# Attention in longer runs of one kind of matmul, earlier loads, an even spread of row transposes in an auction

## The chip, the cores and the metric

The kernel runs on one core of a Trainium2 chip. The metric is the time of one execution on the device, in microseconds (us); lower is better. The five engines work side by side and are tied together by semaphores: TensorE (PE in the rows; PEld is its weight load), VectorE (DVE), ScalarE (ACT), GpSimd (POOL) and SyncE (SP), which issues most of the DMAs.

## The reference, cut to what matters

```python
def _attn_ref(q, k, v):                     # 4 batches, 12 heads, 448 positions, 64 wide
    scores = scale * np.matmul(q, k.transpose(0, 1, 3, 2)) - np.log(S)
    attn = 1.0 / (1.0 + np.exp(-scores))
    return np.matmul(attn, v)

def _moe_ref(x, w_gate, w1, w2):            # 1792 tokens of 768, 8 experts of 1024
    logits = x @ w_gate
    # all (token, expert) pairs in falling order of logit: a token goes to the expert of the first
    # pair at which it is free and the expert has fewer than 224 tokens
    ...
    out[mask] = np.maximum(x[mask] @ w1[e], 0.0) @ w2[e]

def _moe2_ref(x, w_in, w_out, s, b):        # one dense layer, 768 to 2048 and back
    r = np.maximum(x @ w_in, 0.0)
    return (s * (r * r) + b) @ w_out
```

The three run one after the other, in float32.

## The kernel before, in words

Three stages follow each other. **Attention** fills the first 181 us. Heads go in pairs: 4 batches of 6 pairs make 24 pairs, and the pair number i runs from 0 to 23. For a pair the kernel loads `rk` and `rq` (keys and queries, transposed; `load_qk`) and `vt` (values; `load_v`). The 448 keys are cut into 4 chunks `c` of 112. For a chunk PE makes two score matmuls, one for each head, into a two-bank tile `psc` (line 237; 64 contraction rows and 112 output columns of the array each, and the two heads use the upper and the lower half of its rows), and ACT takes the sigmoid into `attn` (line 238). The product with the values adds the 4 chunks up in one bank `pv` (line 243; 112 rows and 64 columns, the two heads use the two halves of the columns), and ACT copies it to `xT` (line 252). A matmul of float32 is two instructions on PE, so "x8" in a row is four matmuls.

The function `scores_av(n, i, mid)` makes the scores of pair n = i + 1 and the values of pair i together. It alternates: the scores of two chunks (four matmuls), then the values of two chunks (four matmuls), and so once more. One call is called a round here. The callback `mid` puts the router's small matmuls between: `gate` (line 259) adds up the logits of a batch in the bank `plg`, ACT copies them to `lg` (line 264), `gate_turn` (line 271) turns them into the bank `pt`, and `prefs` on DVE (lines 280 to 287) copies them to `L` and ranks them. In the last batch `bracket` finds the range of the logits in three stages, with two more small matmuls (lines 297 and 303) into `plg`.

Beside that, DVE narrows the second layer's weights from int64 pairs to float32: `convert` is four DVE instructions (lines 155 to 158) on one of 32 pieces, `CONV[i]` of them after round i. A piece is loaded into one of three buffers `craw`, and its result `co` (three buffers too) is stored to `nw` one conversion later. In the last four rounds ACT and POOL split the first pieces of the experts' weights (`w_high`, line 187; `w_low`, line 198).

All these loads and stores are issued by SP, in the order of the program. A load waits on SP until its buffer is free, and everything behind it waits too. The loads of pair i + 3 (q, k) and i + 2 (v) are issued at round i.

**The auction** (181 to 217 us) gives tokens to experts: `STEPS` = 10 steps of prices, each a chain DVE (`aw`), PE (`pa`), DVE (`LM`), comparisons on DVE and on ACT (line 456), PE (`pb`), DVE (`jd`). PE and ACT use the gaps to turn `xT` into rows: one turn is four transposes into `px` (line 409), an ACT copy to `xrow` (line 416) and a store to `xs` (line 417). There are 24 turns: one before the steps, `ROWS[it]` in each step, and what is left in `places`, which builds the lists `idx` of tokens (matmuls of line 525, and line 529). The first `SYNC` = 4 turns are stored from ACT's queue, the rest from SP's. **The experts** and the dense layer take the rest, from a gather of the rows (line 539) on.

Of the kernel before, what the change touches and what calls it, by code (L numbers as in the profile page):

```python
# [8 lines left out]
F32 = mybir.dt.float32  # L9
# [15 lines left out]
CP = 112  # L25
# [12 lines left out]
MORE = (3, 8)  # L38
AHEAD = (2, 3, 4, 5)
WARM = (9, 10)  # L40
ROWS = (2, 2, 2, 3, 3, 3, 2, 2, 2, 2)
SYNC = 4
SIGNS = 2
CONV = [1, 1, 2, 1, 2] * 4 + [1, 2, 1]
FULL = CAP - 0.5
BIG = 1.0e30
FLATC = 16384.0
# [14 lines left out]
def tile_kernel(ctx, tc, qT, kT, v, wg, w1, w2, wi, wo, s2, b2, cst, out):  # L62
# [53 lines left out]
    cgp = early.enter_context(tc.tile_pool(name="cgp", bufs=1))  # L116

    att = ExitStack()
    qk = att.enter_context(tc.tile_pool(name="qk", bufs=4))
    vp = att.enter_context(tc.tile_pool(name="vp", bufs=2))  # L120
    at = att.enter_context(tc.tile_pool(name="at", bufs=2))
    ps_s = att.enter_context(tc.tile_pool(name="ps_s", bufs=2, space=PSUM))
    ps_v = att.enter_context(tc.tile_pool(name="ps_v", bufs=2, space=PSUM))
    ps_l = att.enter_context(tc.tile_pool(name="ps_l", bufs=1, space=PSUM))


# [20 lines left out]
    def convert():  # L147
        if not coming:
            return
        i = coming.pop(0)  # L150
        r = craw.pop(i)
        lo, hi = r[:, :, 0], r[:, :, 1]
        b = cgp.tile([128, 768], I32, name="cb_", bufs=2)
        a = cgp.tile([128, 768], I32, name="co", bufs=3)
        V.tensor_scalar(a, hi, 3, 0x3FFFFFFF, op0=ALU.logical_shift_left, op1=ALU.bitwise_and)
        V.tensor_scalar(b, lo.bitcast(U32), 2.0 ** -29, None, op0=ALU.mult)
        V.scalar_tensor_tensor(a, hi, -(1 << 30), a, op0=ALU.bitwise_and, op1=ALU.bitwise_or)
        V.tensor_tensor(a, a, b, op=ALU.add)
        cout.append((i, a))
        cv_out(1)  # L160
        cv_in()
# [47 lines left out]

    def load_v(i):  # L210
        b, p = pairs[i]
        vt[i] = vp.tile([CP, NC, 128], F32, name="vt", bufs=4)
        nc.sync.dma_start(vt[i], v[b, p])

    def load_qk(i):
# [4 lines left out]
        nc.sync.dma_start(rq, qT[b, p])  # L220
        raw_qk[i] = (rq, rk)

    def scores_av(n, i, mid):
        if n is not None:
            rq, rk = raw_qk.pop(n)
            attn[n] = at.tile([CP, 2, NC, S], F32, name="attn")
        if i is not None:
            a = attn.pop(i)
            pv = ps_v.tile([128, 512], F32, name="pv")
        for c2 in range(0, NC, 2):  # L230
            for c in (c2, c2 + 1):
                mid(c)
                if n is not None:
                    p = ps_s.tile([CP, 2, 512], F32, name="psc")
                    for j in range(2):
                        me = slice(j * D, (j + 1) * D)
                        T.matmul(p[:, j, :S], rk[me, c * CP:(c + 1) * CP], rq[me], start=True, stop=True)  # L237
                    A.activation(attn[n][:, :, c, :], p[:, :, :S], AF.Sigmoid, bias=nls[:CP],  # L238
                                 scale=1.0 / math.sqrt(D))
            for c in (c2, c2 + 1):  # L240
                if i is not None:
                    for j in range(2):
                        T.matmul(pv[j * 64:(j + 1) * 64, :S], vt[i][:, c, j * D:(j + 1) * D], a[:, j, c, :],  # L243
                                 start=(c == 0), stop=(c == NC - 1))
        if i is not None:
            b, p = pairs[i]
            xt = xT[:, p, b * S:(b + 1) * S]
            if i == len(pairs) - 1:
                A.copy(xt[:, :2 * CP], pv[:, :2 * CP])
                A.copy(xt[:, 2 * CP:], pv[:, 2 * CP:S])  # L250
            else:
                A.copy(xt, pv[:, :S])

    def gate(b, p0, p1, last):
        if p0 == 0:
            plg[b] = ps_l.tile([128, 512], F32, name="plg")
        for p in range(p0, p1):
            i = p % 4
            T.matmul(plg[b][i * 32:(i + 1) * 32, :S], wgs[:, p], xT[:, p, b * S:(b + 1) * S],
                     start=(p < 4), stop=(p + 4 >= last))  # L260

    def gate_copy(b):
        lgs[b] = at.tile([128, S], F32, name="lg", bufs=1)
        A.copy(lgs[b], plg.pop(b)[:, :S])

    def gate_turn(b, stop):
        lg = lgs.pop(b)
        pt = ps_l.tile([128, 512], F32, name="pt")
        pts[b] = pt[:CP, :NC * E].rearrange("p (c e) -> p c e", e=E)
        for c in range(NC):  # L270
            T.matmul(pts[b][:, c], lg[:, c * CP:(c + 1) * CP], ct[:, C_SEL:C_SEL + E], start=(c == 0),
                     stop=(stop and c == NC - 1))
# [17 lines left out]
    def bracket(stage):  # L290
# [2 lines left out]
            V.tensor_reduce(mm[:CP, 0:1], lv, axis=AX.X, op=ALU.max)  # L293
            V.tensor_reduce(mm[:CP, 1:2], lv, axis=AX.X, op=ALU.min, negate=True)
        elif stage == 1:
            pm = ps_l.tile([128, 512], F32, name="plg")
            T.transpose(pm[:2, :CP], mm[:CP], ident[:CP, :CP])
            m2 = ep.tile([2, 1], F32, name="m2")
            V.tensor_reduce(m2, pm[:2, :CP], axis=AX.X, op=ALU.max)
            V.tensor_scalar(dg, ident[:2, :2], m2, None, op0=ALU.mult)  # L300
        else:
            pr = ps_l.tile([128, 512], F32, name="plg")
            T.matmul(pr[:, :2], on[:2], dg, start=True, stop=True)
            V.tensor_copy(mm, pr[:, :2])
            lb = ep.tile([128, 1], BF16, name="lb")
# [26 lines left out]
    load_v(1)  # L332
    load_qk(2)
    cv_in()
    cv_in()
    cv_in()
    scores_av(0, None, lambda c: None)
    nc.sync.dma_start(sb2[:, 0:1], s2.partition_broadcast(128))
    nc.sync.dma_start(sb2[:, 1:2], b2.partition_broadcast(128))
    G.memset(on, 1.0)  # L340
# [10 lines left out]
    N = len(pairs)  # L351
    for i in range(N):
        b, p = pairs[i]
        if i + 2 < N:
            load_v(i + 2)
        if i + 3 < N:
            load_qk(i + 3)
        def mid(c):
            if b == B - 1 and p == 5:
                if c == 0:  # L360
                    gate(b, 0, 5, 5)
                elif c == 2:
                    gate_copy(b)
                elif c == 3:
                    gate_turn(b, False)
            elif p == 5 and c == 0:
                gate(b, 0, 4, 6)
            elif p == 0 and b and c == 1:
                gate(b - 1, 4, 6, 6)
            elif p == 0 and b and c == 3:  # L370
                gate_copy(b - 1)
            elif p == 1 and b and c == 0:
                gate_turn(b - 1, True)

        scores_av(i + 1 if i + 1 < N else None, i, mid)
        if p == 1 and b:
            prefs(b - 1)
        if b == B - 1 and 2 <= p <= 4:
            bracket(p - 2)
        if N - 6 <= i < N - 2:  # L380
            w_dma()
        if i >= N - 4:
            w_high()
            w_low(G)
        if i < N - 1:
            for _ in range(CONV[i]):
                convert()
    gate_last(B - 1)
    prefs(B - 1)
    cv_out(0)  # L390
# [28 lines left out]
    def rows(n):  # L419
        rows_out(rows_in(n))  # L420

    got = rows_in(1)
    pl = ps_1.tile([128, CP], F32, name="pl")
    T.transpose(pl, L.rearrange("p c e -> p (c e)"), ident[:CP, :CP])
    A.copy(LT, pl)
# [411 lines left out]
```

## Time and profile before

| | us |
|---|---|
| three timed runs | 963.48, 968.11, 972.67 (median 968.11) |
| profiled execution, its own time | 965.9 |
| its span | 964.1 |
| PE busy in the span | 937.4 |
| DVE busy | 563.9 |
| ACT busy | 443.8 |

The span is what the trace covers; the time of the same execution is 1.8 us longer. PE is busy for 97% of the span, but busy on PE only says that a matmul is in the array: how dense these are is read from the distances between them. The clock that PE was granted is 1.00 through attention, 0.50 in most of the auction, and 1.00 again in nearly all of the rest. Times of rows are counted from the start of the span.

### The profile page before, as it was taken

To read this page: it belongs to the slowest core of one execution; us is meant where nothing else is said; L and a number is where in the kernel's file an instruction comes from. 1 tells how busy PE (TensorE), PEld (TensorE's weight loads), DVE (VectorE), ACT (ScalarE), POOL (GpSimd) and SP (SyncE) were. 2 spreads that over 40 slices of the span, in tenths; PEclk is the share of its full clock that TensorE was granted. 3 is DMA by queue.
4 is the path that set the end of the run, shared out by engine and by line. 5 is a ranking of instruction groups with operands and counts; after the bars stand their busy time and mean duration, and the time that the engine had idled before them with its cause. 6 is when DMAs were issued, how large, how long until landed. Compare 5 with 4: busy or idle time off the path is not lost.

```text
span 964.1 us, 14094 instructions
## 1 busy us (share of the span) xinstructions
PE 937.4 (97%) x5277; PEld 782.4 (81%) x5277; DVE 563.9 (58%) x1015; ACT 443.8 (46%) x771; POOL 137.4 (14%) x136
## 2 busy tenths in 40 slices
PE   9999999778999999999999999999999999999997
PEld 3333333466899999999999999999999999999997
DVE  3565635764777774278677321877774278677320
ACT  5666666573564332266533223664332266433220
POOL 1000001223330000153100002430000152100001
PEclk9999999857999999999999999999999999999999
DMA  8999996272674434477443433774434476533411
GB/s 288 380 318 360 351 374 230 98 228 79 208 232 145 124 114 137 131 244 234 142 138 108 127 99 91 262 233 147 118 116 140 131 235 204 152 121 109 119 46 66
DMA packets 68456, 173.08 MB, mean 180 GB/s; under 512 B 7968, under 2 KB 24864, under 8 KB 68384
## 3 DMA queue, kind: packets, MB, share of 16 engines
q1 hardware_dynamic: 64256, 160.22, 51.5%
q0 software_dynamic: 2272, 11.01, 3.3%
q10 hardware_dynamic: 1856, 0.92, 0.3%
q8 instruction: 42, 0.69, 0.3%
q14 instruction: 30, 0.25, 0.1%
HBM read 148.52 MB, written 23.59 MB: 179 GB/s over the span
## 4 chain that ended last, share of the span: by engine, by line
PE 82%; DVE 6%; DMA 5%; issue 3%; ACT 2%; POOL 1%; SPq 1%; POOLq 0%; ACTq 0%; DVEq 0%
PE acc L642 9%; PE acc L708 8%; PE acc L710 8%; PE acc L709 8%; PE acc L759 8%; PE acc L761 8%; PE acc L760 8%; PE pv L243 7%; PE psc L237 7%; PE acc L643 5%; DVE wl L198 2%; DMA raw<-in_w_dram 2%; DMA rq<-in_qT_dram 2%; PE px L409 2%; ACT wh L187 1%
## 5 line engine op out<-in xcount | busy, mean ns | idle before, releaser
L187 ACT CAST wh<-raw 128x768 fp32r<-128x768 f32 (+1 forms) x240 | 209.2, 878 | 160.1 <-PE acc L761 133.8
L198 DVE TENSOR_TENSOR wl<-raw,wh 128x768 fp32r<-128x768 f32 (+1 forms) x198 | 210.5, 1068 | 104.9 <-ACT wh L187 104.9
L198 POOL TENSOR_TENSOR wl<-raw,wh 128x768 fp32r<-128x768 f32 (+1 forms) x42 | 92.1, 2201 | 433.4 <-ACT wh L187 285.2
L759 PE MATMUL acc<-wh,gt 128*128 128x384 f32 x448 | 149.9, 335 | 0.0
L760 PE MATMUL acc<-wl,gt 128*128 128x384 f32 x448 | 149.7, 334 | 0.0
L761 PE MATMUL acc<-wh,gt 128*128 128x384 f32 x448 | 149.6, 334 | 0.0
L708 PE MATMUL acc<-y,wh 128*128 128x448 f32 x384 | 141.4, 368 | 0.0
L710 PE MATMUL acc<-y,wl 128*128 128x448 f32 x384 | 140.6, 366 | 0.0
L709 PE MATMUL acc<-y,wh 128*128 128x448 f32 x384 | 140.6, 366 | 0.0
L642 PE MATMUL acc<-u,wh 128*128 128x448 f32 x384 | 121.7, 375 | 1.7 <-DVE u L666 1.5
L238 ACT ACTIVATE attn<-psc,nls 112x896 f32<-112x896 f32 x96 | 92.1, 1005 | 53.8 <-PE psc L237 53.8
L732 ACT ACTIVATE r<-acc 128x448 f32<-128x448 f32 x64 | 34.9, 545 | 150.9 <-PE acc L710 150.9
L643 PE MATMUL acc<-u,wl 128*128 128x224 f32 x384 | 101.5, 264 | 0.0
L642 PE MATMUL acc<-x,wh 128*128 128x448 f32 x288 | 95.3, 385 | 0.0
L237 PE MATMUL psc<-rq,rk 64*112 64x448 f32 x384 | 85.6, 561 | 1.1 <-ACT attn L238 0.6
L760 PEld LDWEIGHTS acc<-wl,gt 128*128 128x128 f32 x448 | 84.1, 188 | 0.0
L759 PEld LDWEIGHTS acc<-wh,gt 128*128 128x128 f32 x448 | 84.1, 188 | 0.0
L761 PEld LDWEIGHTS acc<-wh,gt 128*128 128x128 f32 x448 | 84.1, 188 | 0.0
L243 PE MATMUL pv<-attn,vt 112*64 112x448 f32 x384 | 82.8, 552 | 0.0
L643 PE MATMUL acc<-x,wl 128*128 128x224 f32 x288 | 77.2, 268 | 2.1 <-POOL wl L198 2.1
L733 DVE SCALAR_TENSOR_TENSOR r<-r,sb 128x448 f32<-128x448 f32 x64 | 43.8, 685 | 60.4 <-ACT r L732 60.3
L642 PEld LDWEIGHTS acc<-u,wh 128*128 128x128 f32 x384 | 72.0, 188 | 8.6 <-DVE u L666 3.3
(214 smaller groups left out, 1245.3 us busy)
## 6 DMA issues: line engine op xcount, KB each, us to landing
raw<-nw SPq DMA_DIRECT2D x128, 384.0 KB, 3.0
raw<-in_w_dram SPq DMA_DIRECT2D x64, 384.0 KB, 3.7
raw<-in_w_dram SPq DMA_DIRECT2D x48, 512.0 KB, 4.4
craw<-in_wi_dram SPq DMA_DIRECT2D x16, 768.0 KB, 7.6
nw<-co SPq DMA_DIRECT2D x32, 384.0 KB, 8.0
craw<-in_wo_dram SPq DMA_DIRECT2D x16, 768.0 KB, 6.9
rk<-in_kT_dram SPq DMA_DIRECT2D x24, 224.0 KB, 9.2
rq<-in_qT_dram SPq DMA_DIRECT2D x24, 224.0 KB, 8.4
```

The lines of the kernel that those rows point to most:

```text
L187: A.copy(h[:, :k], raws[i][:, :k])
L198: eng.tensor_sub(lo[:, :k], r[:, :k], h[:, :k].bitcast(F32))
L237: T.matmul(p[:, j, :S], rk[me, c * CP:(c + 1) * CP], rq[me], start=True, stop=True)
L243: T.matmul(pv[j * 64:(j + 1) * 64, :S], vt[i][:, c, j * D:(j + 1) * D], a[:, j, c, :], start=(c == 0), stop=(c == NC - 1))
L642: T.matmul(p[:, :2 * CAP], wh[:, k], src[:, k].rearrange("p a s -> p (a s)"), start=(k == 0), stop=False)
L643: T.matmul(p[:, :CAP], wl[:, k], src[:, k, 0], start=False, stop=(k == n - 1))
L708: T.matmul(p, wh, src[:, k, 0], start=first, stop=False)
L709: T.matmul(p, wh, src[:, k, 1], start=False, stop=False)
L710: T.matmul(p, wl, src[:, k, 0], start=False, stop=last)
L759: T.matmul(ps[t][:, :DH], hi, wh[:, cols], start=(f == 0), stop=False)
L760: T.matmul(ps[t][:, :DH], hi, wl[:, cols], start=False, stop=False)
L761: T.matmul(ps[t][:, :DH], lo, wh[:, cols], start=False, stop=(f == KG - 1))
```

## The change

Attention is cut into other blocks. `scores_av` becomes `scores(n, c0, c1)` and `values(i)`. A round i now is: all four chunks of values of pair i (eight matmuls, sixteen PE instructions), then the last two chunks of scores of pair i + 1 and the first two of pair i + 2 (eight matmuls). Ahead of the first round stand the whole scores of pair 0 and the first half of pair 1. The router's matmuls come between the scores and the next values: `gate` at the end of the rounds p = 4 and 5, `gate_turn` and `prefs` in the round p = 0 of the next batch (before: p = 1), and `bracket` at p = 1, 2, 3 (before: p = 2, 3, 4).

The PSUM banks go with it: three `psc` tiles instead of two, one `pv` bank instead of two, and one bank `small` for `plg` and `pt` together.

Loads come earlier: q and k four pairs ahead instead of three, v three instead of two, with five buffers each instead of four; q and k now stand ahead of v. To make room, the scratch tile `cb_` of a conversion has one buffer instead of two.

The conversions at the rounds 20, 21 and 22 are 2, 2, 0 instead of 1, 2, 1. In the auction each step makes two turns (eight transposes), where the steps 3, 4 and 5 had three; three turns stand ahead of the steps instead of one, and one turn is left for `places`, where none was.

```diff
-ROWS = (2, 2, 2, 3, 3, 3, 2, 2, 2, 2)
+ROWS = (2, 2, 2, 2, 2, 2, 2, 2, 2, 2)
-CONV = [1, 1, 2, 1, 2] * 4 + [1, 2, 1]
+CONV = [1, 1, 2, 1, 2] * 4 + [2, 2, 0]
-    qk = att.enter_context(tc.tile_pool(name="qk", bufs=4))
+    qk = att.enter_context(tc.tile_pool(name="qk", bufs=5))
-    ps_s = att.enter_context(tc.tile_pool(name="ps_s", bufs=2, space=PSUM))
-    ps_v = att.enter_context(tc.tile_pool(name="ps_v", bufs=2, space=PSUM))
+    ps_s = att.enter_context(tc.tile_pool(name="ps_s", bufs=3, space=PSUM))
+    ps_v = att.enter_context(tc.tile_pool(name="ps_v", bufs=1, space=PSUM))
-        b = cgp.tile([128, 768], I32, name="cb_", bufs=2)
+        b = cgp.tile([128, 768], I32, name="cb_", bufs=1)
-        vt[i] = vp.tile([CP, NC, 128], F32, name="vt", bufs=4)
+        vt[i] = vp.tile([CP, NC, 128], F32, name="vt", bufs=5)
...
+    def scores(n, c0, c1):
+        if n >= len(pairs):
+            return
+        if c0 == 0:
             attn[n] = at.tile([CP, 2, NC, S], F32, name="attn")
+        rq, rk = raw_qk[n]
+        for c in range(c0, c1):
+            p = ps_s.tile([CP, 2, 512], F32, name="psc")
+            for j in range(2):
+                me = slice(j * D, (j + 1) * D)
+                T.matmul(p[:, j, :S], rk[me, c * CP:(c + 1) * CP], rq[me], start=True, stop=True)
+            A.activation(attn[n][:, :, c, :], p[:, :, :S], AF.Sigmoid, bias=nls[:CP], scale=1.0 / math.sqrt(D))
...
+    def values(i):
+        a, v = attn.pop(i), vt.pop(i)
+        pv = ps_v.tile([128, 512], F32, name="pv")
+        for c in range(NC):
+            for j in range(2):
+                T.matmul(pv[j * 64:(j + 1) * 64, :S], v[:, c, j * D:(j + 1) * D], a[:, j, c, :],
+                         start=(c == 0), stop=(c == NC - 1))
...
-    scores_av(0, None, lambda c: None)
+    scores(0, 0, NC)
+    scores(1, 0, 2)
...
-        if i + 2 < N:
-            load_v(i + 2)
+        if i + 4 < N:
+            load_qk(i + 4)
         if i + 3 < N:
-            load_qk(i + 3)
...
+            load_v(i + 3)
+        values(i)
+        scores(i + 1, 2, NC)
+        scores(i + 2, 0, 2)
+        if p == 0 and b:
+            gate_turn(b - 1, True)
             prefs(b - 1)
-        if b == B - 1 and 2 <= p <= 4:
-            bracket(p - 2)
+        elif p == 4:
+            gate(b, 0, 4 if b < B - 1 else 5, 6 if b < B - 1 else 5)
+            if b == B - 1:
+                gate_copy(b)
+        elif p == 5 and b < B - 1:
+            gate(b, 4, 6, 6)
+            gate_copy(b)
+        if b == B - 1 and 1 <= p <= 3:
+            bracket(p - 1)
...
+    gate_turn(B - 1, False)
     gate_last(B - 1)
...
-    got = rows_in(1)
+    got = rows_in(3)
```

How the instructions stand is shown at three places. The first is PE at the border between two batches. Before:

```order
L237 MATMUL psc<-rq,rk 112x448 x4
L243 MATMUL pv<-attn,vt 64x448 x4
L237 MATMUL psc<-rq,rk 112x448 x2
L259 MATMUL plg<-xT,wgs 32x448 x2
L237 MATMUL psc<-rq,rk 112x448 x2
L243 MATMUL pv<-attn,vt 64x448 x4
```

Four score matmuls and four value matmuls alternate, and the second part of `gate` cuts a run of scores in two. Now, at the same border on PE:

```order
L233 MATMUL psc<-rq,rk 112x448 x8
L258 MATMUL small<-xT,wgs 32x448 x4
L243 MATMUL pv<-attn,vt 64x448 x8
L233 MATMUL psc<-rq,rk 112x448 x8
L258 MATMUL small<-xT,wgs 32x448 x2
L243 MATMUL pv<-attn,vt 64x448 x8
```

Runs are eight matmuls long, and the router's matmuls stand only where the kind changes anyway.

The second place is SP from its ninth load on, at the start of attention (`craw` is a piece to convert, `sb` two scalars of the last layer). Before:

```order
L218 DMA rk<-in_kT_dram 128x448
L220 DMA rq<-in_qT_dram 128x448
L139 DMA craw<-in_wi_dram 128x1536 x3
L338 DMA sb_76<-in_s_dram 128x1
L339 DMA sb_76<-in_b_dram 128x1
L213 DMA vt<-in_v_dram 112x512
L218 DMA rk<-in_kT_dram 128x448
L220 DMA rq<-in_qT_dram 128x448
```

The queries of pair 2 come first here, and those of pair 3 last, behind three pieces and the scalars. Now, from the same load on SP:

```order
L218 DMA rk<-in_kT_dram 128x448
L220 DMA rq<-in_qT_dram 128x448
L139 DMA craw<-in_wi_dram 128x1536
L218 DMA rk<-in_kT_dram 128x448
L220 DMA rq<-in_qT_dram 128x448
L213 DMA vt<-in_v_dram 112x512
L139 DMA craw<-in_wi_dram 128x1536 x2
L340 DMA sb_76<-in_s_dram 128x1
```

The loads of pair 3 have moved ahead of two of the pieces.

The third place is ACT between attention and the auction's first comparisons (`LT` is the table of logits, `junk` a comparison). Before:

```order
L425 COPY LT<-pl 128x112
L416 COPY xrow<-px 112x512
L417 DMA xs<-xrow 112x4x128
L456 ACTIVATE junk_114,cnt<-LM,dv_94 128x112
L456 ACTIVATE junk_114,cnt<-LM,th 128x112
```

One turn's copy and store stand ahead of the comparisons. Now, on ACT:

```order
L421 COPY LT<-pl 128x112
L412 COPY xrow<-px 112x512
L413 DMA xs<-xrow 112x4x128
L412 COPY xrow<-px 112x512
L413 DMA xs<-xrow 112x4x128
L412 COPY xrow<-px 112x512
L413 DMA xs<-xrow 112x4x128
L452 ACTIVATE junk_114,cnt<-LM,dv_94 128x112
```

Three turns' copies and stores stand there.

## Rows read from the trace of the kernel before

**Rows 1.** Windows: us, busy of PE, PEld, DVE, ACT, POOL, clock, DMA share, GB/s

```profile
109.00:136.00 27.00, 27.00 (x134) 9.01 (x136) 17.29 (x25) 17.19 (x20) 0.00 (x0) 1.00 1.02 378
...
190.00:200.00 10.00, 8.38 (x42) 7.35 (x42) 5.97 (x50) 7.88 (x26) 2.40 (x6) 0.50 0.72 204
```

**Rows 2.** The chain of waits in attention: start, length, engine and line

```profile
50.68 0.94 PE psc L237 x4
51.62 0.88 PE plg L259 x4
...
66.01 1.69 PE psc L237 x8
67.70 1.65 PE pv L243 x8
```

**Rows 3.** Timeline of PE and ACT at the start: start, length, what, idle before

```profile
5.67 1.90 ACT L238 ACTIVATE attn<-psc,nls 112x896 f32<-112x896 f32 x2 [3.44 <-PE psc L237]
...
8.84 1.91 PE L237 MATMUL psc<-rq,rk 64*112 64x448 f32 x8 [0.21 <-ACT attn L238]
...
10.68 1.72 PE L243 MATMUL pv<-attn,vt 112*64 112x448 f32 x8
...
22.96 1.76 PE L237 MATMUL psc<-rq,rk 64*112 64x448 f32 x8 [0.53 <-DMA rq<-in_qT_dram]
```

**Rows 4.** Timeline of PE and ACT in a steady round

```profile
15.68 1.76 PE L237 MATMUL psc<-rq,rk 64*112 64x448 f32 x8
15.79 0.53 ACT L252 COPY xT<-pv 128x448 f32<-128x448 f32 x1 [0.50 <-PE pv L243]
...
16.80 1.91 ACT L238 ACTIVATE attn<-psc,nls 112x896 f32<-112x896 f32 x2 [0.47 <-PE psc L237]
```

**Rows 5.** Waits: who waited for whom, us in total, times, longest

```profile
DVE co L155 <- DMA nw<-co: 30.9, 12, 5.4
...
DVE L L280 <- PE pt L271: 23.4, 3, 10.4
```

**Rows 6.** Timeline of PE, DVE and POOL at the end of attention

```profile
173.29 1.69 PE L259 MATMUL plg<-xT,wgs 128*32 128x448 f32 x10 [0.77 <-DVE mm L304]
...
175.68 0.55 DVE L155 TENSOR_SCALAR co<-craw 128x768 int32<-128x768 int32 x1
...
177.60 0.96 DVE L158 CUSTOM_DVE_ANT_0 co<-co,cb__1363 128x1536 uint16<-128x1536 uint16 x1
...
179.62 0.95 PE L276 MATMUL pt<-wgs,xT 128*112 128x8 f32 x8 [0.45 <-ACT xT L249]
...
180.61 0.19 DVE L280 COPY L<-pt 112x32 f32<-112x32 f32 x1 [2.05 <-PE pt L276]
180.62 1.80 POOL L198 TENSOR_TENSOR wl<-raw,wh 128x768 fp32r<-128x768 f32 x1 [5.21 <-ACT wh L187]
180.83 1.87 DVE L284 TENSOR_TENSOR ge<-L 112x256 f32<-112x256 f32 x1
```

**Rows 7.** Timeline of DVE: the same ranking two batches earlier

```profile
59.58 0.42 DVE L284 TENSOR_TENSOR ge<-L 112x256 f32<-112x256 f32 x1
```

**Rows 8.** The chain of waits in the auction

```profile
190.69 1.89 PE px L409 x8
...
193.67 2.74 PE px L409 x12
```

**Rows 9.** Timeline of ACT at the auction's first step

```profile
183.41 0.58 ACT L416 COPY xrow<-px 112x512 f32<-112x512 f32 x1 [1.89 <-DVE Wp L287]
...
184.02 0.35 ACTq L417 DMA_DIRECT2D xs<-xrow  x1
...
184.81 0.39 ACT L456 ACTIVATE junk<-LM,dv 128x112 bf16<-128x112 f32 x1 [0.82 <-DVE LM L452]
```

**Rows 10.** Timeline of PE and POOL from the auction's end to the gather

```profile
219.87 2.64 PE L525 MATMUL pi<-R,oh 112*128 112x16 bf16 x32
...
223.14 1.18 POOL L539 DMA_INDIRECT xr<-xs,idx  x1 [4.65 <-DVE idx L529]
```

More of the change, by code (lines that the diff above doesn't have):

```diff
@@ L221, in load_qk @@
         raw_qk[i] = (rq, rk)
-    def scores_av(n, i, mid):
-        if n is not None:
-            rq, rk = raw_qk.pop(n)
+    def scores(n, c0, c1):
+        if n >= len(pairs):
+            return
+        if c0 == 0:
             attn[n] = at.tile([CP, 2, NC, S], F32, name="attn")
[L227 to L252, printed above, removed]
@@ new lines, in scores @@
+        rq, rk = raw_qk[n]
[5 more added lines that the diff above has]
+            A.activation(attn[n][:, :, c, :], p[:, :, :S], AF.Sigmoid, bias=nls[:CP], scale=1.0 / math.sqrt(D))
+        if c1 == NC:
+            raw_qk.pop(n)
+    def values(i):
[5 more added lines that the diff above has]
+                         start=(c == 0), stop=(c == NC - 1))
+        b, p = pairs[i]
+        xt = xT[:, p, b * S:(b + 1) * S]
+        if i == len(pairs) - 1:
+            A.copy(xt[:, :2 * CP], pv[:, :2 * CP])
+            A.copy(xt[:, 2 * CP:], pv[:, 2 * CP:S])
+        else:
+            A.copy(xt, pv[:, :S])
@@ L254, in gate @@
     def gate(b, p0, p1, last):
         if p0 == 0:
-            plg[b] = ps_l.tile([128, 512], F32, name="plg")
+            plg[b] = ps_l.tile([128, 512], F32, name="small")
         for p in range(p0, p1):
@@ L267, in gate_turn @@
         lg = lgs.pop(b)
-        pt = ps_l.tile([128, 512], F32, name="pt")
+        pt = ps_l.tile([128, 512], F32, name="small")
         pts[b] = pt[:CP, :NC * E].rearrange("p (c e) -> p c e", e=E)
@@ L295, in bracket @@
         elif stage == 1:
-            pm = ps_l.tile([128, 512], F32, name="plg")
+            pm = ps_l.tile([128, 512], F32, name="small")
             T.transpose(pm[:2, :CP], mm[:CP], ident[:CP, :CP])
@@ L301, in bracket @@
         else:
-            pr = ps_l.tile([128, 512], F32, name="plg")
+            pr = ps_l.tile([128, 512], F32, name="small")
             T.matmul(pr[:, :2], on[:2], dg, start=True, stop=True)
@@ L334, in tile_kernel @@
     cv_in()
+    load_qk(3)
+    load_v(2)
     cv_in()
     cv_in()
-    scores_av(0, None, lambda c: None)
+    scores(0, 0, NC)
+    scores(1, 0, 2)
     nc.sync.dma_start(sb2[:, 0:1], s2.partition_broadcast(128))
@@ L353, in tile_kernel @@
         b, p = pairs[i]
-        if i + 2 < N:
-            load_v(i + 2)
+        if i + 4 < N:
+            load_qk(i + 4)
         if i + 3 < N:
-            load_qk(i + 3)
[L358 to L376, printed above, removed]
-            prefs(b - 1)
-        if b == B - 1 and 2 <= p <= 4:
-            bracket(p - 2)
+            load_v(i + 3)
[4 more added lines that the diff above has]
+            gate_turn(b - 1, True)
+            prefs(b - 1)
+        elif p == 4:
[7 more added lines that the diff above has]
+            bracket(p - 1)
         if N - 6 <= i < N - 2:
```

## The prediction, made blind

> **What bounds the kernel now.** I read the windows first, to see which engine fills which stage. In attention TensorE is busy for every microsecond at a granted clock of 1.00 (2.4 GHz), while VectorE and ScalarE are busy for 17 of 27 us, and the DMA engines are full as well (share 1.02, 378 GB/s); in the auction no engine is full and the clock is 0.50, or 1.2 GHz [rows 1]. So attention has two candidates, TensorE and the DMAs, and the list of waits tells them apart. VectorE, which lives on the loads and stores of the conversions, waited 23.4 us in three waits for TensorE to deliver logits [rows 5]: at each border of a batch the conversions were done early. TensorE waited 0.53 us for a load, once [rows 3]. Attention is bound by TensorE, and the DMAs have room on average, though little within a batch.
>
> The chain of waits then shows how dense TensorE's work is. A run of four score matmuls takes 1.69 us, one of four value matmuls 1.65. Where the router's matmuls cut a run of scores in two, each half takes 0.94 [rows 2]. Two halves make 1.88, not 1.69: starting a run costs 0.94 + 0.94 - 1.69 = 0.19 us, and two matmuls within it 0.75. The values have as many columns, so their start costs 1.65 - 2 x 0.75 = 0.15 us.
>
> **Longer runs.** Values: 24 rounds with two runs each become one each, 24 starts less, 24 x 0.15 = 3.6 us. Scores: after the opening run there were 45 runs, and three of them were cut by the router (45 + 3 = 48 starts); now there are 22 of eight matmuls and one of four. That is 25 less, 25 x 0.19 = 4.75 us. The router's own matmuls stay as many and still stand at a change of kind. Sum: **-8.35 us**.
>
> What could take the place of these starts is ScalarE. In a round it needs four sigmoids at 0.95 and a copy at 0.53, 4.35 us [rows 4], against a round of 1.65 + 1.50 + 1.69 + 1.50 = 6.34 us, so it is no bound. But the fourth score tile of a run needs the first of three tiles back. The first sigmoid starts 16.80 - 15.68 = 1.12 us behind the scores [rows 4] and ends 0.95 later, at 2.07; by TensorE's count the fourth tile starts at 0.19 + 3 x 0.75 = 2.44, or at 2.25 if the start's cost lies at the run's end. Room of 0.2 to 0.4 us; I cost it at nothing. The single `pv` bank is free 0.5 us behind its run and needed 3 us later. The one bank `small` is free when the ranking has copied it, and asked for again rounds later, or, in the last batch, a round behind each stage of `bracket`; that costs nothing while VectorE keeps up. The one buffer `cb_` is written and read by VectorE alone, in order, and costs nothing.
>
> The Trainium skill speaks against such a change in "TensorEngine Tiling (Array Packing)", section "PSUM Bottleneck": once tiling has sped up the matmuls, emptying PSUM may become the bottleneck. By that rule the fourth tile of each run would wait, which is the first rival below; the trace shows such a wait only in the opening, with two tiles.
>
> **The opening.** With two tiles TensorE waited for ScalarE there: the scores that start at 8.84 wait for a tile, and the first values start at 10.68 [rows 3]. With three, the sixth tile needs the third sigmoid, done at 5.67 + 1.90 + 0.95 = 8.52, and the values follow 0.94 later, at 9.46: **-1.2 us** (0 if the second pair's load lands late, which no row shows). The queries of pair 3, which came behind three pieces and cost 0.53 us at 22.96 [rows 3], now stand ahead of two of them: **-0.5 us**. The later loads are asked for a round earlier; nothing waited for them before, so they gain nothing, and cover the faster rounds. A queue that carries the same bytes per round in 6.3 instead of 6.7 us needs 378 x 6.7 / 6.3 = 402 GB/s where it ran at 378 [rows 1]; it has that room only because the 23.4 us are there to catch up.
>
> **The end of attention.** Before the last values, TensorE waited 0.77 us for VectorE to free the router's bank, since `bracket` stands behind two conversions, and 0.45 us for the last copy to `xT` [rows 6]. Now `bracket` comes a round earlier and `gate_turn` covers the copy: **-1.2 us**.
>
> The conversions get tighter. From the third ranking (end of round 18) to the last copy to `L`, TensorE needs three rounds (19.0), half a round with the gate (3.15 + 1.69 + 1.62), the last values 3.15 and the router 0.88 + 0.96: about 31 us. VectorE has in the same time the ranking (about 1.3: 0.19, 0.42 and two more such), seven conversions of 178.56 - 175.68 = 2.9 us [rows 6], and `bracket` (about 3.5: 2.4 from 173.29 to 175.68 for its last stage [rows 6], and two short ones): 25 us, and it must wait for TensorE twice between. By my count of those waits 3 us are left behind the last conversion, against 2.05 us of waiting before [rows 6]. So "no conversion in the last round" by itself frees nothing. GpSimd's splits of weights now fall beside the last conversions, and this costs: the ranking took 1.87 us beside such a split [rows 6] and 0.42 without one [rows 7]. Three hits of about 1.45 us are 4.4, against the 3 us: **+0.5 us** taken, 0 to 3 for the range.
>
> The Trainium skill has this in "GPSIMD Engine Reference", section "1. Specifications": GpSimd shares its SBUF interfaces with VectorE and contends with VectorE instructions that read two inputs from SBUF. By that rule the add of a conversion, which reads two, suffers and the other three may not; the sum would then hold one hit for each split, as taken.
>
> Attention together: -8.35 - 1.2 - 0.5 - 1.2 + 0.5 = **-10.75 us**.
>
> **The auction.** Steps 3 to 5 hang on twelve transposes, 2.74 us; eight take 1.89, and are the longest part of their step as well [rows 8]. Three steps gain 3 x 0.85 = **-2.55 us**. The clock is 0.50 with twelve transposes already [rows 1], so fewer have nothing to lose there.
>
> The two turns that moved ahead are not free. Their transposes lie under the ranking, but ScalarE has to copy and store three turns ahead of the first comparison. One copy with its store takes 0.58 + 0.35 us and began at 183.41, behind the ranking; the comparison began at 184.81, after 0.82 us without other work [rows 9]. Two more are 1.9 us; about 0.7 of it fits where ScalarE is idle, because the copies need no longer wait for the ranking. **+1.2 us** (0 to 1.9).
>
> The last turn now lies in `places`. Its four transposes, about 0.95 us at the low clock (half of eight at 1.89 [rows 8]), stand on TensorE ahead of the 32 matmuls of line 525, which took 2.64 us and end what the gather waits for [rows 10]; the copy and store behind them also come due about then. **+0.9 us** (0 to 1.5). Auction together: **-0.45 us**.
>
> **How the numbers follow.** -10.75 - 0.45 = -11.2 us. The profiled execution took 965.9 us (its span and 1.8 us), so its successor takes 954.7. The median of the runs is 2.2 us above it and gives 956.9. I take the middle, **955.8 us**. 1% of the median is 9.7 us, about what a measurement of this kernel can tell from no change, so the forecast is not far beyond that bound.
>
> **First rival: the fourth score tile waits for ScalarE.** The 0.2 us of room may be too little. The wait in the opening was 0.21 us each [rows 3]; 22 times is 4.6 us, and the time is 960.4. For it: the sigmoids take 0.95 against 0.75 for a tile. Against it: the room counted above.
>
> **Second rival: the run is not what costs.** If eight value or score matmuls take twice what four take, the 8.35 us stay and the time is 964.1. For it: no run of eight stands alone in the rows. Against it: 0.94, twice, against 1.69 [rows 2].
>
> **Third rival, slower: the conversions become the bound at the end.** Behind round 18 VectorE has seven of them, where each must find its result buffer stored. The stores cost 30.9 us in 12 waits [rows 5], 2.6 each, longest 5.4. With 2.6 in each of the seven they take 5.5, the stretch takes 1.3 + 38.5 + 3.5 = 43.3 instead of 31 us, and all but the gain is lost: about 968. Above 2.6 us each the kernel is slower than before; with 4 us it takes 978. Against it: no load of queries or keys is left behind round 19, and no new piece behind round 20, so the queue empties just then. With waits in two or three of the seven the loss is 3 to 7 us and the time 959 to 963.
>
> **Chances.** Forecast 0.62; first rival 0.14; second 0.08; third in its mild form 0.10, in its slow form 0.06. The forecast's own bounds are 950 to 960: its three uncertain costs (0 to 3, 0 to 1.9 and 0 to 1.5 us) at either end, and 1.1 us to either anchor. For 8 in 10 I reach to the first rival and the mild third: **949.5 to 963**. Faster by over 1% 0.62, within 1% 0.33, slower 0.05.
>
> **What will show it.** A round of about 6.3 us in the chain, with runs of about 3.19 (scores) and 3.15 (values); first values near 9.5 us; no wait of TensorE for `rq`; the copy to `L` near 170 us instead of 180.61; steps of the auction alike at about 3 us, the first near 4; the gather about 0.9 us later behind the last step. Wrong would be: a wait of TensorE for ScalarE in each run of scores, runs of eight at 3.3 us or more, waits for loads behind a batch's border, or a last conversion that ends behind the router's last matmul.

## The result, and the profile of the changed kernel

The changed kernel took **954.68 us** (median of 4, 952.91 to 956.67) against 966.97 (median of 4, 963.48 to 972.67): a ratio of 0.987, 95% interval 0.9836 to 0.9905. It is 1.3% faster; the forecast was 955.8. Its profiled execution took 956.25 us, with a span of 954.5.

The windows, in the columns of [rows 1]. TensorE is busy throughout, as before, and the DMAs as full; VectorE has its work in less time (19.19 of 27 us, where it was 17.29).

```profile
103.00:130.00 27.00, 27.00 (x142) 10.09 (x140) 19.19 (x27) 17.65 (x22) 0.00 (x0) 1.00 1.02 380
180.00:190.00 10.00, 8.08 (x42) 6.67 (x42) 6.92 (x58) 7.34 (x26) 2.86 (x8) 0.50 0.76 221
```

The chain of waits in attention, which answers [rows 2]. A run is now eight matmuls (16 instructions), and takes 3.16 us (values) and 3.19 (scores); the forecast had 3.15 and 3.19:

```profile
104.73 3.16 PE pv L243 x16
107.88 3.19 PE psc L233 x16
```

The timeline of PE and ACT at the start ([rows 3]). The first sigmoid is 0.97 us later than before, the first values only 0.24 us earlier. A wait for `rq` is not there any more. The matmuls into `psc<-zero` are the kernel's warm-up of TensorE; before, they took 3.49 us:

```profile
1.19 3.49 PE L320 MATMUL psc<-zero 128*112 128x512 bf16 x9 [1.19 <-DVE zero L316]
```

Now:

```profile
1.19 4.09 PE L319 MATMUL psc<-zero 128*112 128x512 bf16 x9 [1.19 <-DVE zero L315]
5.20 5.31 PE L233 MATMUL psc<-rq,rk 64*112 64x448 f32 x24
...
6.64 5.50 ACT L234 ACTIVATE attn<-psc,nls 112x896 f32<-112x896 f32 x6 [4.41 <-PE psc L233]
...
10.44 3.23 PE L243 MATMUL pv<-attn,vt 112*64 112x448 f32 x16
```

The waits that answer [rows 5]: both are a little smaller.

```profile
DVE co L155 <- DMA nw<-co: 27.2, 12, 5.1
DVE L L279 <- PE small L270: 21.3, 3, 10.5
```

The timeline of PE, DVE and POOL at the end of attention ([rows 6]). TensorE waits for nothing there; the last conversion, slowed beside the split that GpSimd began at 166.53, ends at 169.62, and the copy to `L` stands at 170.01, where it was at 180.61. Before, VectorE waited 2.05 us for it, now 0.40.

```profile
163.46 1.69 PE L258 MATMUL small<-xT,wgs 128*32 128x448 f32 x10
...
166.53 2.27 POOL L198 TENSOR_TENSOR wl<-raw,wh 128x768 fp32r<-128x768 f32 x1 [4.03 <-ACT wh L187]
167.16 2.46 DVE L158 CUSTOM_DVE_ANT_0 co<-co,cb__1341 128x1536 uint16<-128x1536 uint16 x1
169.05 0.93 PE L275 MATMUL small<-wgs,xT 128*112 128x8 f32 x8
169.76 1.80 POOL L198 TENSOR_TENSOR wl<-raw,wh 128x768 fp32r<-128x768 f32 x1 [0.96 <-ACT wh L187]
170.01 0.19 DVE L279 COPY L<-small 112x32 f32<-112x32 f32 x1 [0.40 <-PE small L275]
170.24 1.60 DVE L283 TENSOR_TENSOR ge<-L 112x256 f32<-112x256 f32 x1
```

The auction in the timeline: ScalarE's third store ahead of the first comparison ([rows 9]), three choices (`aw`), and the end with the turn left over ([rows 10]). The first step, from the choice at 173.01 to the next at 176.52, takes 3.51 us; each later one 2.98 to 3.0. The gather begins 212.16 - 203.41 = 8.75 us behind the last choice; before it was 223.14 - 216.28 = 6.86 ([rows 10] has the gather, the last line here the choice before).

```profile
173.01 0.33 DVE L427 SCALAR_TENSOR_TENSOR aw<-LT,dv,pb 128x112 bf16<-128x112 f32 x1 [0.50 <-PE pb L423]
...
174.30 0.31 ACTq L413 DMA_DIRECT2D xs<-xrow  x1
174.66 0.39 ACT L452 ACTIVATE junk<-LM,dv 128x112 bf16<-128x112 f32 x1 [0.39 <-DVE junk L460]
176.52 0.34 DVE L427 SCALAR_TENSOR_TENSOR aw<-LT,dv,WT 128x112 bf16<-128x112 f32 x1
...
203.41 0.34 DVE L427 SCALAR_TENSOR_TENSOR aw<-LT,dv,WT 128x112 bf16<-128x112 f32 x1
...
207.90 1.90 PE L521 MATMUL pi<-R,oh 112*128 112x16 bf16 x32
208.14 0.58 ACT L412 COPY xrow<-px 112x512 f32<-112x512 f32 x1 [2.60 <-PE px L405]
209.95 0.24 DVE L525 SCALAR_TENSOR_TENSOR idx<-pi,ia 128x8 int32<-128x8 f32 x2 [0.64 <-ACT ia L524]
212.16 1.18 POOL L535 DMA_INDIRECT xr<-xs,idx  x1 [6.54 <-issue]
```

```profile
216.28 0.34 DVE L431 SCALAR_TENSOR_TENSOR aw<-LT,dv,WT 128x112 bf16<-128x112 f32 x1
```

So 10.98 us are won at the gather (223.14 to 212.16), and 9.6 in the span of these two executions. The 1.4 us between lie in two transfers that took longer in this one: TensorE had all of the first gather 6.64 us behind its start (218.80; 5.90 before, 229.04), and a reload of weights in the chain of waits (265.29; before 275.67) took 4.47 us, where it took 3.69. No instruction of theirs was changed; the medians differ by 12.3 us.

### The profile page after: what moved, and what is told of

Same layout as the page of the kernel before. It is cut to its first block, busy times and chain, and to the rows that moved or that the text cites. A ratio compares the mean times of both kernels' runs of the same rounds, so it can differ in the third digit from the quotient of the medians.

```text
span 954.5 us, 14092 instructions
## 1 busy us (share of the span) xinstructions
PE 927.2 (97%) x5277; PEld 784.2 (82%) x5277; DVE 564.8 (59%) x1015; ACT 440.7 (46%) x771; POOL 136.9 (14%) x136
## 4 chain that ended last, share of the span: by engine, by line
PE 86%; DVE 5%; DMA 4%; issue 3%; ACT 2%; POOL 1%; POOLq 0%; ACTq 0%; SPq 0%; DVEq 0%
PE acc L638 11%; PE acc L704 8%; PE acc L705 8%; PE acc L706 8%; PE psc L233 8%; PE acc L755 8%; PE acc L757 8%; PE acc L756 8%; PE pv L243 8%; PE acc L639 5%; DMA raw<-in_w_dram 3%; DVE wl L198 2%; PE px L405 2%; DMA xr<-xs,idx 1%; ACT wh L187 1%
## 5 line engine op out<-in xcount | busy, mean ns | idle before, releaser
L234 ACT ACTIVATE attn<-psc,nls 112x896 f32<-112x896 f32 x96 | 88.9, 1008 | 13.8 <-PE psc L233 13.8
L233 PE MATMUL psc<-rq,rk 64*112 64x448 f32 x384 | 78.9, 550 | 0.0
L243 PE MATMUL pv<-attn,vt 112*64 112x448 f32 x384 | 77.5, 545 | 0.0
```

Of the source, the lines that this page charges most:

```text
L243: T.matmul(pv[j * 64:(j + 1) * 64, :S], v[:, c, j * D:(j + 1) * D], a[:, j, c, :], start=(c == 0), stop=(c == NC - 1))
```

## The experiments

All are compared with the kernel before, on the same chip each time (medians of before 966.1 to 967.1). Since the first sigmoid stands anywhere from 5.67 to 7.09 us in these profiles, with the old opening and with the new, the stage is measured in each profile from ScalarE's first sigmoid to the copy to `L`: 180.61 - 5.67 = 174.94 us before, 170.01 - 6.64 = 163.37 in the changed kernel.

| kernel | time, us | ratio to before (95%) | first sigmoid to `L`, us |
|---|---|---|---|
| changed | 954.68 | 0.987 (0.9836 to 0.9905) | 163.37 |
| att_only | 954.93 | 0.9867 (0.9843 to 0.989) | 163.37 |
| auction_only | 967.17 | 0.9999 (0.9984 to 1.0014) | 174.35 |
| runs_of_four | 962.94 | 0.9959 (0.9946 to 0.9973) | 170.96 |
| runs_of_two | 988.32 | 1.024 (1.0211 to 1.0268) | 197.20 |
| two_tiles | 972.62 | 1.007 (1.0044 to 1.0096) | 181.31 |
| lead_undone | 965.45 | 1.0001 (0.998 to 1.0022) | 174.66 |
| lead_qk_only | 956.41 | 0.9898 (0.9881 to 0.9914) | 167.92 |
| lead_undone_pool | 960.15 | 0.9935 (0.9919 to 0.9952) | 165.14 |
| lead_undone_act | 974.21 | 1.0082 (1.0065 to 1.0099) | 182.48 |
| conv_last | 956.19 | 0.9907 (0.9885 to 0.9929) | 166.71 |
| rest_early | 952.28 | 0.9845 (0.9818 to 0.9872) | 163.37 |

### Attention alone, the auction alone

`att_only` is the changed kernel with

```diff
-ROWS = (2, 2, 2, 2, 2, 2, 2, 2, 2, 2)
+ROWS = (2, 2, 2, 3, 3, 3, 2, 2, 2, 2)
-    got = rows_in(3)
+    got = rows_in(1)
```

> Attention as changed, the auction as it was (23 turns in steps of two and three, one turn ahead, none left over). My theory: the whole gain is attention's, and the auction's part nets about nothing (42.5 us from the copy to L to the gather before, 42.2 in the changed kernel). It expects the copy to L at 170 us, the gather 42.5 us behind it at 212.5, twelve transposes of 2.74 us in three steps, and a time within 0.5 us of the changed kernel (954.7), ratio 0.987. Rival: the auction's shorter steps carry about 2 us of the gain. It expects about 956.9, ratio 0.9895.

`auction_only` is the kernel before with the reverse of that edit.

> Attention as it was, the auction as changed. My theory: the first step is 0.7 us later, four steps are shorter by 2.9 in sum, the turn left over costs 1.84; sum -0.4 us: gather at 222.8, time 966.6, ratio 0.9996, the same within what can be measured. Rival: the store of the left-over turn is late in the changed kernel only because other transfers are in its way there; then the gather comes 2.2 us earlier than before, at 221, and the time is 964.8, ratio 0.998.

Measured: 954.93 us with attention's part and 967.17 with the auction's. From the copy to `L` to the gather it is 212.69 - 170.40 = 42.29 us with the old auction, 42.15 with the new one, 43.26 in `auction_only` (181.44 to 224.70; its first step took 4.35 us there). The whole gain is attention's, as the theory of `att_only` has it. In `auction_only` the time is the same as before, but the stage is 43.26 - 42.53 = 0.73 us longer and not 0.4 shorter; its rival, a gather 2.2 us earlier, is out. The first step tells the two apart: it takes 4.35 us where ScalarE's first copy began behind the ranking (`auction_only`, `lead_undone`, `lead_undone_pool`), and 3.5 to 3.8 where it began ahead of it, as in the changed kernel (3.51). `auction_only` also shows the old opening with a late first sigmoid, at 7.09, in its timeline:

```profile
7.09 1.91 ACT L238 ACTIVATE attn<-psc,nls 112x896 f32<-112x896 f32 x2 [4.86 <-PE psc L237]
...
12.10 1.73 PE L243 MATMUL pv<-attn,vt 112*64 112x448 f32 x8
```

The first values stand 12.10 - 7.09 = 5.01 us behind it, as in [rows 3] (10.68 - 5.67 = 5.01); with three tiles it is 10.44 - 6.64 = 3.80.

### The length of a run

`runs_of_four` puts `values(i, 0, 2)`, the scores of the rest of one pair, `values(i, 2, NC)` and the scores of half the next in place of the changed kernel's two blocks; `runs_of_two` cuts once more:

```diff
-        values(i, 0, 2)
-        scores(i + 1, 2, NC)
-        values(i, 2, NC)
-        scores(i + 2, 0, 2)
+        values(i, 0, 1)
+        scores(i + 1, 2, 3)
+        values(i, 1, 2)
+        scores(i + 1, 3, NC)
...
```

> The changed kernel, with the values cut in two and the scores between the halves, so that TensorE changes between scores and values every four matmuls again; three score tiles, the earlier loads and everything else stay. My theory: 24 starts of values at 0.15 and about 23 of scores at 0.19 come back, 8 us: copy to L at 178, runs of 1.65 to 1.69 in the chain, time 962.5 to 963, ratio 0.9955. Rival: the third score tile and the earlier loads carry the gain, not the length of a run: copy to L at 170 to 171, time 955.

> The changed kernel with values and scores alternating every two matmuls: twice the starts of the kernel with runs of four. My theory, that each start of a run costs 0.15 us (values) or 0.19 (scores) whatever its length: 48 more starts of values and about 46 of scores than with four, 15.9 us: runs of 0.90 (values) and 0.94 (scores) in the chain, copy to L at 194, time 978.9. Rival: the cost falls with the length of the run, or hides behind other work of the changed kernel; then the time stays below 970.

The chain of waits of `runs_of_four` in mid attention:

```profile
104.87 1.69 PE psc L233 x8
106.56 1.65 PE pv L246 x8
```

The same view of `runs_of_two`:

```profile
103.84 0.90 PE pv L246 x4
104.75 0.94 PE psc L233 x4
```

Runs of two, four and eight score matmuls take 0.94, 1.69 and 3.19 us: 0.19 and 0.375 for each matmul, at every length. Runs of values, 0.90, 1.65 and 3.16, give 0.15 in the same way. Attention got 7.6 us longer with runs of four (8 expected) and the time 8.3; the rival falls. With runs of two it got 26.2 us longer than with four, not 15.9: the time of a run was right, and a wait came on top that I had not counted, 8.0 of the 10.3 us that are missing (the other 2.3 stay open). With one `pv` bank, the next pair's first values stand one short run behind the last, and ScalarE's copy is late, in the waits of `runs_of_two`:

```profile
PE pv L246 <- ACT xT L256: 8.0, 13, 0.7
```

What a start is made of, the weight loads of the changed kernel suggest:

```profile
107.81 0.27 PEld L233 LDWEIGHTS psc<-rq,rk 64*112 64x112 f32 x4 [0.70 <-issue]
108.28 0.18 PEld L233 LDWEIGHTS psc<-rq,rk 64*112 64x112 f32 x2 [0.20 <-issue]
...
111.01 0.20 PEld L243 LDWEIGHTS pv<-attn,vt 112*64 112x64 f32 x4 [0.67 <-issue]
```

Within a run the weights of the next matmul are loaded while one runs, with gaps of 0.20 us. At a change of kind none is loaded ahead: the loads stop for 0.70 or 0.67 us and begin again with the run. One load takes 0.172 us for scores and 0.136 for values (means from 20 to 160 us), and a start costs 0.19 and 0.15. So a start looks like the one load that nothing covers; no run tried this by itself.

### The third score tile

```diff
-    ps_s = att.enter_context(tc.tile_pool(name="ps_s", bufs=3, space=PSUM))
+    ps_s = att.enter_context(tc.tile_pool(name="ps_s", bufs=2, space=PSUM))
```

> The changed kernel with two score tiles instead of three. My theory, by the count of the prediction: the third tile of a run needs the first sigmoid's end at 2.07 us and could start at 1.69 (0.38 of waiting), the fourth needs the second's at 3.02 and could start at 2.82 (0.20); 0.58 in each of 22 runs of eight, 12.8 us: copy to L at 183, time 967.5, as slow as before. So the third tile is what lets the long run pay. Rival: ScalarE's sigmoids have no part in it; the time stays at 955.

972.62 us: slower than before. One run in the timeline of PE and its weight loads:

```profile
105.01 1.76 PE L233 MATMUL psc<-rq,rk 64*112 64x448 f32 x8
...
107.12 1.91 PE L233 MATMUL psc<-rq,rk 64*112 64x448 f32 x8 [0.35 <-ACT attn L234]
108.02 0.27 PEld L233 LDWEIGHTS psc<-rq,rk 64*112 64x112 f32 x4 [0.62 <-ACT attn L234]
```

The run takes 108.96 - 105.01 = 3.95 us instead of 3.19, 0.76 more and not 0.58. The third tile starts at 107.12 and the fourth at 108.02, each about 0.1 us behind the end of the sigmoid that frees its banks, as expected; but the fourth then takes 0.94 us, as a run of two does, and not 0.75. Its weights, too, are loaded only when the wait is over, so a run that a wait interrupts pays its start again. 22 runs make 16.7 us, the opening 1.2 more; 17.94 were measured. With three tiles the same place shows no idle of TensorE at all; the chain has runs of 3.19.

This is also where the Trainium skill ("TensorEngine Tiling (Array Packing)", section "PSUM Bottleneck") comes true in this kernel: emptying PSUM is the bottleneck of a run of eight with two tiles (0.76 us a run), and is not with three (no wait).

### The loads

```diff
-        if i + 4 < N:
-            load_qk(i + 4)
-        if i + 3 < N:
-            load_v(i + 3)
+        if i + 2 < N:
+            load_v(i + 2)
+        if i + 3 < N:
+            load_qk(i + 3)
```

(with four buffers for each, and without the two loads added ahead of the loop).

> The changed kernel with the loads as late as before (queries and keys three pairs ahead in four buffers, values two ahead in four). My theory: the earlier loads earn little, since queries asked for at the start of one round are used 1.75 rounds, 11 us, later and land in 8.7 us at the median: waits of TensorE for loads of 0.5 to 2 us in all, time 955.2 to 956.7. Rival: the rounds are so much faster that without the lead TensorE waits at many rounds; over 4 us, time above 959.

My theory fell: 965.45 us, nearly the whole gain lost. The timeline shows TensorE waiting for queries four times, 7.3 us in all; the longest wait, and the run of values behind it:

```profile
115.18 3.33 PE L233 MATMUL psc<-rq,rk 64*112 64x448 f32 x8 [3.31 <-DMA rq<-in_qT_dram]
118.44 4.57 PE L243 MATMUL pv<-attn,vt 112*64 112x448 f32 x16
```

The half run of scores took 3.33 us instead of 1.69 and the values 4.5 instead of 3.16, and the granted clock was 0.50 behind the wait (windows, in the columns of [rows 1]): 3 us more.

```profile
111.00:115.00 4.00, 0.87 (x6) 0.13 (x2) 2.20 (x3) 1.91 (x2) 0.00 (x0) 0.92 1.04 347
115.00:118.50 3.50, 3.32 (x10) 1.22 (x10) 2.36 (x4) 1.01 (x1) 0.00 (x0) 0.50 1.04 336
```

Why the queries were late stands in the timeline of SP and DVE ahead of that. SyncE issues in order; from 95.08 to 103.85 it issued nothing, since VectorE waited for the logits of a batch and the next loads and stores of conversions waited for VectorE. The queries that were needed at 111.87 could be asked for only at 108.04. The kernel before stood still as long (139.42 to 148.47 in its timeline of SP) and no load came late: there queries were used two rounds of 6.68 us behind their request, 13.4 us, and in this order 1.75 rounds of 6.35, 11.1.

```profile
95.08 0.33 SPq L145 DMA_DIRECT2D nw<-co  x1
...
100.70 0.19 DVE L279 COPY L<-small 112x32 f32<-112x32 f32 x1 [11.57 <-PE small L270]
...
103.85 0.33 SPq L139 DMA_DIRECT2D craw<-in_wo_dram  x1
...
108.04 0.43 SPq L220 DMA_DIRECT2D rq<-in_qT_dram  x1
```

Three more runs tell the queue from the distance, and one lead from the other. `lead_qk_only` undoes the values' lead alone. `lead_undone_pool` undoes both, and the loop's `load_qk` goes to `nc.gpsimd` in place of `nc.sync`; `lead_undone_act` sends it to `nc.scalar`.

> The changed kernel with the values' loads as late as before; queries and keys keep the longer lead. The run before showed 10.8 us lost when both leads are undone, and TensorE waiting for queries alone (7.35 us in four waits, and about 3 us at the low clock behind the longest of them). New theory: the lead of queries and keys is what is needed, since they are now used half a round earlier; that of the values is not. It expects no wait for queries, copy to L at 170 to 170.5, time 954.7. Rival: the queue is short as a whole, and the later values delay the rest; then TensorE waits for values or queries and the time is 957 or more.

> Both leads undone, as in the run that took 965.45 us, but the queries and keys of the loop are asked for from GpSimd's queue, not SyncE's. Theory A, the queue: SyncE issues in order, and from 95.08 to 103.85 it issued nothing, since stores of conversions stood ahead that waited for VectorE, which waited 11.57 us for the logits; the loads behind them came a round late. From an idle queue they come on time: copy to L at 170 to 172, time 955 to 957. Theory B, the distance: 1.75 rounds are too short at a full DMA; the waits stay and the time is 962 to 966.

> The same from ScalarE's queue, which is in order behind the sigmoids but never behind a conversion. Theory A, the queue: copy to L at 170 to 172; two issues of about 0.4 us a round fit in ScalarE's 2 us of room a round, time 955 to 957. Theory B, the distance: time 962 to 966.

In `lead_undone_pool` TensorE waits for no queries. Attention takes 165.14 us: of the 11.3 lost 9.5 came back, so what was late is the request behind the stalled queue, not the distance. The transfers did not get faster: a load of `rq` lands 7.3 us behind its issue at the median, and 7.1 in `lead_undone`. The rest is two waits for values, 1.63 us. The time is 960.15, above what I expected, though: its first step of the auction took 4.36 us instead of 3.51 and its first gather waited for the last store until 214.71, 42.7 us behind the copy to `L` instead of 42.15; about 2 us behind the gather I can't account for. In its timeline, GpSimd asks while SyncE stands still:

```profile
97.02 0.54 POOL L220 DMA_DIRECT2D rq<-in_qT_dram  x1
```

`lead_undone_act` fits neither theory: 974.21 us. An issue held ScalarE up, as its timeline shows: 6 us between the load of `rk` and that of `rq`, and the copy behind them 4.86 us late. The buffer was not what it waited for: the pair that had it before was done with it the round before last. TensorE waits for ScalarE here, 12.5 us in six waits, and for no load.

```profile
85.00 0.33 ACTq L218 DMA_DIRECT2D rk<-in_kT_dram  x1
...
90.99 0.34 ACTq L220 DMA_DIRECT2D rq<-in_qT_dram  x1
91.37 0.53 ACT L251 COPY xT<-pv 128x448 f32<-128x448 f32 x1 [4.86 <-DMA craw<-in_wi_dram]
```

`lead_qk_only` took 956.41 us, between its two theories: no wait for queries, but three for values, 1.83, 0.49 and 0.32 us. Behind the first, at 24.66, a run took 4.92 us instead of 3.16, at a granted clock of 0.66. These waits and that run make 4.4 of the 4.55 us that attention lost in the profile, but the profiled execution was the slowest of the four (959.56); by the medians the lead of the values is worth 1.7 us. That of the queries should be most of the other 9; no run undid it alone.

### The conversion in the last round

```diff
-CONV = [1, 1, 2, 1, 2] * 4 + [2, 2, 0]
+CONV = [1, 1, 2, 1, 2] * 4 + [1, 2, 1]
```

> The changed kernel with one of its conversions moved back from round 20 into attention's last round. My theory: with one conversion less ahead of the last stage of bracket VectorE comes there 2.0 us before TensorE's matmul for it (158.30 to 158.68), waits, and has three conversions behind it instead of two; the copy to L comes 1.7 to 3.1 us later, time about 957. What the moved conversion earns is that wait. Rival, the prediction's own step: the sum of VectorE's work is the same, so it is worth nothing, 954.7.

956.19 us, and 3.3 us more of attention. Of these 2.4 are left at the gather (207.92 us behind the first sigmoid against 205.52), since the ranking, behind the splits now, was not slowed. In the timeline of DVE `bracket` waits for TensorE, and the copy to `L` comes straight behind a conversion:

```profile
157.91 0.16 DVE L303 COPY mm<-small 128x2 f32<-128x2 f32 x1 [1.23 <-PE small L302]
...
166.52 2.17 DVE L155 TENSOR_SCALAR co<-craw 128x768 int32<-128x768 int32 x1
...
169.09 2.56 DVE L157 SCALAR_TENSOR_TENSOR co<-craw,co 128x768 int32<-128x768 int32 x1
...
172.55 0.18 DVE L279 COPY L<-small 112x32 f32<-112x32 f32 x1
```

So the sum of VectorE's work is not all that counts. A conversion ahead of `bracket` fills a wait there (1.23 us; none in the changed kernel); behind it, it lies at the end, beside GpSimd's splits, each of which slows an operation by 1.5 to 1.6 us. In three rows (167.16 in the changed kernel, 166.52 and 169.09 here) the operation ends about 0.13 us less than its own length behind the split's end (168.80, 168.27, 170.83), as if it did its work only when the split is over.

### The turn left over, and ScalarE's stores

```diff
-SYNC = 4
+SYNC = 0
...
+        rest()
         for c in range(NCH):
...
                 full(pk)
-                rest()
```

> The changed kernel with two edits of the auction: the left-over turn's transposes, copy and store stand ahead of the sixteen comparisons of slots instead of behind the sixth, and every store to xs is issued by SyncE, none by ScalarE. My theory: the gather waits for the landing of the left-over turn's store, not for the 0.95 us of its transposes, and the first step for ScalarE's copies and issues: the gather comes 6.9 us behind the last choice instead of 8.70 (-1.8), the first step takes 2.8 to 3.0 us instead of 3.51 (-0.6): gather 2.4 us earlier, at 209.8, time 952.3 against 954.7. Rival: the transposes ahead of the 32 small matmuls are what costs, wherever they stand; the gather then comes at most 0.6 us earlier, time 954.

The gather, in the timeline of POOL, begins 210.12 - 203.20 = 6.92 us behind the last choice, and it waits for `idx`, not for a store:

```profile
210.12 1.18 POOL L535 DMA_INDIRECT xr<-xs,idx  x1 [4.70 <-DVE idx L525]
```

The first step takes 2.93 us (173.42 to 176.35): ScalarE's three copies take 1.56 us together, where with their stores between them they took 2.6. From the copy to `L` to the gather it is 39.75 us against 42.15, the 2.4 us that were expected. The transposes are not what cost: the 32 small matmuls behind them still end with VectorE's comparisons. 952.28 us is the fastest median of all, 14.9 us under the kernel before; the 2.4 us to the changed kernel are clear in the trace, while the intervals of the two ratios overlap.

## Why the prediction was right

**What bounds the kernel: right.** TensorE bounds attention, in the rows before and after.

**Longer runs, -8.35: right.** Undoing them alone gave back 7.6 us of attention and 8.3 of the time; runs of four have three starts of scores fewer than the old order, 0.6 us. The second rival (0.08) is out: the start costs the same at three lengths.

**No wait for ScalarE: right.** The first rival (0.14) is out, and `two_tiles` shows what it would have been.

**The opening, -1.2: right, and hidden in the profiles.** Measured from the first sigmoid it is 5.01 - 3.80 = 1.21 us. It shows as 0.24 because the warm-up took 4.09 us in one execution and 3.49 in the other, and the first sigmoid then came 1.44 us behind the first scores instead of 1.06. "First values near 9.5 us" was wrong for that reason.

**The loads, "gain nothing, and cover the faster rounds": half right.** They gain only the 0.5 us for `rq` (a wait in the profile of before, not in that of `auction_only`). But I took the cover for spare room, and expected later that undoing it costs 0.5 to 2 us; it costs 10.8. The order by blocks uses queries a quarter of a round sooner behind their request, in shorter rounds, and the queue stands still for about 9 us at the border of a batch. The list of waits named this stall ([rows 5], 10.4 us), and I read it as room for VectorE without asking what SyncE does in it.

**The end of attention, -1.2: right.** Neither wait is there. Opening, `rq` and end were to give 2.9 us together; `runs_of_four`, which keeps them, is 3.4 to 4.0 us shorter in attention than the two profiles with the old one; with its three starts fewer, 3.5 were to be expected. All of attention, forecast at -10.75, is 10.98 to 11.57 us shorter, counted from the first sigmoid.

**The last conversions, +0.5: too much by 0.5.** Three operations between 154 and 170 us were slowed, by 1.50, 1.37 and 1.50 us, as counted; the room was larger than the 3 us that were counted, and the conversions still ended 0.40 us ahead of the logits here, and 0.1 in `att_only`. So the hits cost nothing, by a small margin. That "no conversion in the last round" by itself frees nothing was wrong: `conv_last` shows it to be worth 2.4 us at the gather (the medians differ by 1.5, with intervals that overlap). The third rival, in which stores end the conversions, did not come. I took the add alone of a conversion's four operations as exposed to a split. The rows of `conv_last` differ: line 155, with one input, took 2.17 us instead of 0.55, and line 157, with two, 2.56 instead of 0.95. The Trainium skill ("GPSIMD Engine Reference", section "1. Specifications") names, beside instructions with two SBUF inputs, those in VectorE's 2-port performance mode, which I had left out. Line 157 agrees with the first; that line 155 ran in that mode no row here shows.

**The auction: the sum right within 0.1, by luck.** Forecast -0.45, measured 42.15 - 42.53 = -0.38, with two terms off against each other. From the copy to `L` to the first choice it is 3.00 us instead of 3.26, which I had not counted. Behind the first step, nine steps gave 2.7 us rather than 2.55 (203.41 - 176.52 = 26.9 against 216.28 - 186.68 = 29.6). The first step, with three copies ahead, took 3.51 us against 186.68 - 183.87 = 2.81: 0.70 rather than 1.2, and in `auction_only` 1.5. The term that was mis-sized is the turn left over: 8.75 - 6.86 = 1.89 us, beyond my bound of 1.5. I had counted its transposes, "about 0.95 us at the low clock"; what the gather waited for was its store, issued at 208.75, where stores of this stretch land 2.3 to 5.1 us behind their issue. The lists were done at 210.19 and the gather began 1.97 us later; before, it was 0.24.

**The whole.** The time, 954.68 against 955.8, owes part of its closeness to such errors against each other. The forecast's "own bounds" are also off: its three costs at either end and 1.1 us to the anchors give 952.1 to 960.7, not 950 to 960.

## What to carry to other kernels

Where TensorE alternates between two kinds of matmul, read the price of a start from a run that happens to be cut, and lengthen the runs as far as PSUM tiles let the emptying engine keep up: one tile too few costs more than the whole gain. A longer run also moves the first use of its inputs forward; before calling a load early enough, look for the longest stretch in which its queue issues nothing, and what stands ahead of it there. The last store ahead of a gather costs its landing, not the work that makes it.

## What the runs showed of the hardware

A wait of 3.31 us of TensorE cost 3 us more behind it (`lead_undone`): the granted clock went from 1.00 to 0.50 (2.4 to 1.2 GHz) for the next half run of scores, and was 0.70 over the run of values behind that. The length of the wait is not all that decides: behind one of 1.83 us (`lead_qk_only`, at 24.66) the clock was 0.66 over the next 5 us, and behind one of 1.87 (`lead_undone`, at 167.52) it stayed at 1.00. And an issue of a load is not always the 0.33 us that its row shows: where the DMAs were full (share 1.04 from 85 to 91 us in `lead_undone_act`), ScalarE stood 6 us between two issues, and the work behind them waited. That full DMAs are what holds the issue is my reading; no run tried it.
